# Seven-product pairs at the even places of a job in the second layer of a Fourier, MoE, MoE kernel

## The chip, the cores and the metric

The kernel runs on one core of a Trainium2 chip. The metric is the device time of one execution in microseconds; lower is better.

## What is computed

Two sequences of 3,008 tokens with 256 features go through a Fourier layer (a real FFT along the sequence, a complex 256x256 product with a soft threshold, the inverse FFT). The 6,016 tokens that come out pass two gated layers of the same shape, and the change is in the second of them alone:

```python
h = x @ w_in            # 6016x256 @ 256x2048
relu6 = np.clip(h + 3.0, 0.0, 6.0)
g = h * relu6 / 6.0
return (g @ w_out).astype(np.float32)   # 6016x2048 @ 2048x256
```

The first layer is alike, with `g = h * np.cos(h)`.

## The kernel before

**Precision.** Every fp32 operand is held as a high part (rounded to fp32r) and a low part (the rest). One product of two operands is three matmuls: high weight with high and with low tokens, low weight with high tokens (`three`, L899).

**Jobs and steps.** Each layer is six jobs of tokens (`HALF`: two halves t of 512 tokens each, in the last job 448), and each job is eight steps q = 0 to 7. A step k (0 to 47 in the first layer, 48 to 95 in the second, job jj = k // 8) makes 256 of the 2,048 hidden features for both token halves: four blocks, `ba`, `bd`, `be`, `bc` by feature half f and token half t. The hidden product `x @ w_in` is done with seven products instead of eight (the `mm` calls, 21 matmuls a step), in four PSUM banks `ha` to `hd`. The elementwise work on a block in the second layer is: ACT makes `r` = relu(h + 3) from PSUM (L856), DVE makes `r` = min(r, 6) * h (L864), ACT rounds it to `gh` (L889), POOL or DVE subtracts, `gl` = r - gh (L177 on POOL, L933 on DVE). Between them DVE adds a shared intermediate `p5` to `hb` to get `hd` and `hc` (`add`, L913).

**The output product** accumulates in four PSUM banks a job, `acc{job}_{t}{d}`, for token half t and output half d. An ordinary step costs 24 matmuls for it: four blocks, two output halves, three matmuls. PSUM has two buffers for each d, so the banks of a job are those of the job before, free only after that job's sums were read.

**Seven-product pairs.** At some places the output product of one step's four blocks is done with seven products instead of eight, 21 matmuls instead of 24. `SEVEN` names the places (q = 1, 3, 5 of the second layer's jobs after its first: 15 of them). The work of such a place is spread over three steps. In the *opening* step (E in the code) the blocks' gates are run and the sums of blocks t0 to t2 are formed on DVE (`less`, tile `sums`); in the *closing* step (O) come the sum t3, the high and low parts of the four sums (ACT `sums_hi` L979, POOL `sums_lo` L177) and four of the seven products; three more come in the *tail*, at the head of the step after (P). One product (V4, `old.into`, L1211) goes straight into an accumulator; the four named X1, X2, X3, X5 serve more than one output: each goes to a PSUM bank of its own (`part`, L1003) and DVE keeps its running sum in SBUF tiles `part0` to `part3` (`keep`, L1008). At the end of a job four additions on POOL (`parts_sum`, L1015) combine these tiles, and `finish` (L1024) reads each accumulator once, adds its tile (`o` at L1042) and stores it.

The weights of the seven products are combined once by the converter (`convert`, `pieces`) and stored to DRAM (`ws_dram`); `load_ring` (L949) brings them back for each pair, into halves of the `wo` tiles that the pairs leave unused.

**Order.** The order of the whole loop is written out by hand: each engine runs its instructions in the order in which the code in the step loop (L1132) issues them, with semaphores between engines. `operands` (L457) prepares the next job's tokens in twelve small stages, spread over the steps (`advance`); in the second layer its subtractions `tok` and `st` run on POOL, for job 7 on DVE. `flush` calls `finish` for each half job that has ended.

Of the kernel before, what the change touches and what calls it, by code (L numbers as in the profile page):

```python
# [54 lines left out]
OPERANDS = (1, 2, 2, 2, 2, 3)  # L55
SEVEN = (1, 3, 5)
V11, V12, V22, V1, V2, V3, V4 = range(7)
# [69 lines left out]
def fourier_moe_moe_kernel(ctx, tc, x, w_r, w_i, b_r, b_i, ta, tg, fg, win1, wout1, win2, wout2, out):  # L127
# [54 lines left out]
    w32 = {}  # L182

    def convert(kind, m, c, k):
# [48 lines left out]
        def sums():  # L233
            if kind == "i" and k == 1:
                w = w32[m, c]
                pooled(pool_add, w[:, S1], w[:, A21], w[:, A22])
                pooled(pool_sub, w[:, S3], w[:, A11], w[:, A21])
                yield
                pooled(pool_sub, w[:, S2], w[:, S1], w[:, A11])
                pooled(pool_sub, w[:, S4], w[:, A12], w[:, S2])  # L240
                yield
            if seven and k == 1:
                w = w32[m, c].rearrange("p s f -> p (s f)")[:, :1024].rearrange("p (s f) -> p s f", f=128)
                a11, a21 = a[:, 256:384], a[:, 384:512]
                pooled(pool_add, w[:, V1], a21, w[:, V22])
                pooled(pool_sub, w[:, V3], a11, a21)
                yield
                pooled(pool_sub, w[:, V2], w[:, V1], a11)
                pooled(pool_sub, w[:, V4], w[:, V12], w[:, V2])
                yield  # L250

        def pieces():
# [17 lines left out]
            def store(z, e, cut, rest):  # L270
                for h, t in ((0, cut), (1, rest)):
                    if z < n:
                        sp.dma_start(at[:, h, z:e], f32(t))
                        if seven and k == 0:
                            sp.dma_start(ws_dram[c][:, h, 128:384], f32(t)[:, 1])
                        elif seven:
                            sp.dma_start(ws_dram[c][:, h, 0:128], f32(t)[:, 1, 0:128])
                    else:
                        sp.dma_start(ws_dram[c][:, h, 384:896], f32(t).rearrange("p a f -> p (a f)"))

            if seven and k == 0:
                act.activation(w32[m, c].rearrange("p s f -> p (s f)")[:, 128:384], a[:, 256:512], AF.Copy)
            lows, stores = [], []
            for z in list(range(0, n, 2)) + [2] * (seven and k) + [None, None]:
# [3 lines left out]
                if lows:  # L288
                    low(*lows[0][2:5])
                    if not direct:  # L290
                        stores.append((*lows[0][:2], lows[0][2], lows[0][4]))
                    lows.pop()
                if z is not None:
                    e = min(z + 2, n) if z < n else z + 2
                    part = src[:, z:e] if z < n else w32[m, c][:, 0:4].rearrange("p s f -> p (s f)")[:, 384:896].rearrange("p (s f) -> p s f", f=256)
                    if direct:
# [534 lines left out]
    with tc.manual_schedule(engines=engines):  # L831
# [103 lines left out]
        def seven_at(k):  # L935
            jj, q = divmod(k, STEPS)
            return jj > NJ and q in SEVEN

# [3 lines left out]
        def ring(p, i):  # L942
            if p % 2 == 0 or i < 2:
                return wo_sb[1, i + 4 * (p % 2)][:, :, 1]
# [18 lines left out]
        class Seven:  # L963
# [59 lines left out]

        def finish(jj, t):  # L1024
# [4 lines left out]
            for d in range(2):  # L1029
                a = acc.pop((jj, t, d))  # L1030
# [7 lines left out]
                else:  # L1038
                    to = out[d * 128 : (d + 1) * 128, STARTS[p] + t * n : STARTS[p] + (t + 1) * n]
                    if jj > NJ:  # L1040
                        by = shared()[2][((X1, X3), (X2, X5))[t][d]]
                        dve.scalar_tensor_tensor(o[:, :n], a[:, :n], 1.0 / 6.0, by[:, :n], op0=ALU.mult, op1=ALU.add)  # L1042
                    elif d == 0:
                        act.activation(o[:, :n], a[:, :n], AF.Copy, scale=1.0 / 6.0)
                    else:
                        dve.tensor_scalar(o[:, :n], a[:, :n], 1.0 / 6.0, None, op0=ALU.mult)
                    sp.dma_start(to, o[:, :n])
# [11 lines left out]
        def w_loads(k):  # L1059
# [72 lines left out]
        for k in range(2 * G):  # L1132
            n = HALF[k // STEPS % NJ]
            a, b, c, d = (bank(z, f"h{r}_{k}") for z, r in zip((0, 1, 2, 3) if k % 2 == 0 else (0, 3, 2, 1), "abcd"))
            E, O, P = (k >= i and seven_at(k - i) for i in range(3))
            ba, bd, be, bc = (Block(k, f, t, h) for f, t, h in ((0, 0, a), (0, 1, d), (1, 0, b), (1, 1, c)))

# [215 lines left out]
```

## Time and profile before

| | |
|---|---|
| median of 3 runs | 1145.98 us (1145.41 to 1146.14) |
| the profiled execution | 1145.05 us, its span 1143.3 us |
| PE (matmul) busy | 1135.4 us, 99% of the span, 5300 instructions |
| DVE, ACT, POOL busy | 865.8, 837.4, 850.2 us (76%, 73%, 74%) |
| mean granted TensorE clock | 0.999 |
| second layer | from 661 us to the end |

A row of the timeline has the start and the duration in us, the engine, the line of kernel.py, the operation, out<-in by the program's names without numbers, the shape and the count of equal instructions in a row; in brackets stands how long the engine had been idle before, and what ended that. A tile named `h` with a letter, `acc` or, as output of a matmul, `part` lies in PSUM; all others lie in SBUF.

### The profile page before, as it was taken

To read this page: it belongs to the slowest core of one execution; us is meant where nothing else is said; L and a number is where in the kernel's file an instruction comes from. 1 tells how busy PE (TensorE), PEld (TensorE's weight loads), DVE (VectorE), ACT (ScalarE), POOL (GpSimd) and SP (SyncE) were. 2 spreads that over 40 slices of the span, in tenths; PEclk is the share of its full clock that TensorE was granted. 3 is DMA by queue.
4 is the path that set the end of the run, shared out by engine and by line. 5 is a ranking of instruction groups with operands and counts; after the bars stand their busy time and mean duration, and the time that the engine had idled before them with its cause. 6 is when DMAs were issued, how large, how long until landed. Compare 5 with 4: busy or idle time off the path is not lost.

```text
span 1143.3 us, 16265 instructions
## 1 busy us (share of the span) xinstructions
PE 1135.4 (99%) x5300; PEld 953.5 (83%) x5300; DVE 865.8 (76%) x1261; ACT 837.4 (73%) x1600; POOL 850.2 (74%) x696
## 2 busy tenths in 40 slices
PE   9999999999999999999999999999999999999998
PEld 7888887778888888888889988888888888888897
DVE  5888877886978888888888676666667577576676
ACT  4787788778888888878888876576666567566564
POOL 3557747876987896987887876558867967868764
PEclk9999999999999999999999999999999999999999
DMA  9656968436103023113215520032031041121210
GB/s 230 189 144 176 269 187 304 142 94 207 63 21 134 28 74 120 42 37 134 65 51 196 195 84 19 15 106 65 1 131 40 12 128 33 42 92 34 69 33 33
DMA packets 67621, 115.48 MB, mean 101 GB/s; under 512 B 7488, under 2 KB 41456, under 8 KB 67024
## 3 DMA queue, kind: packets, MB, share of 16 engines
q1 hardware_dynamic: 67408, 114.30, 31.8%
q8 instruction: 42, 0.69, 0.3%
q14 instruction: 43, 0.35, 0.1%
q10 hardware_dynamic: 128, 0.15, 0.0%
HBM read 73.52 MB, written 40.89 MB: 100 GB/s over the span
## 4 chain that ended last, share of the span: by engine, by line
PE 92%; POOL 2%; DVE 1%; DMA 1%; ACT 1%; issue 1%; SPq 0%; POOLq 0%; ACTq 0%
PE acc L901 38%; PE hb L901 16%; PE ha L901 11%; PE pp L657 6%; PE hc L901 5%; PE hd L901 5%; PE part L901 3%; PE bp L686 3%; PE zp L560 2%; POOL gl L177 1%; PE yp L420 1%; PE vp L725 1%; DMA u_dram<-v 1%; DMA x_big<-in_x_dram 1%; POOL st L481 0%
## 5 line engine op out<-in xcount | busy, mean ns | idle before, releaser
L177 POOL TENSOR_TENSOR gl<-r,gh 128x512 fp32r<-128x512 f32 (+1 forms) x337 | 442.6, 1332 | 133.8 <-ACT gh L889 122.6
L901 PE MATMUL acc<-gh,wo 128*128 128x512 f32 (+1 forms) x1342 | 467.0, 386 | 0.0
L901 PEld LDWEIGHTS acc<-gh,wo 128*128 128x128 f32 x1342 | 252.0, 188 | 46.8
L901 PE MATMUL acc<-gl,wo 128*128 128x512 f32 (+1 forms) x671 | 259.0, 386 | 0.6 <-POOL gl L177 0.5
L901 PE MATMUL hb<-tok,wi 128*128 128x512 f32 (+1 forms) x864 | 241.1, 387 | 0.6 <-DVE hd L913 0.6
L889 ACT ACTIVATE gh<-r 128x512 fp32r<-128x512 f32 (+1 forms) x354 | 210.8, 616 | 4.7 <-DVE r L864 2.4
L901 PEld LDWEIGHTS hb<-tok,wi 128*128 128x128 f32 x864 | 160.7, 188 | 32.1 <-DVE hd L913 2.1
L875 ACT ACTIVATE r<-r 128x512 f32<-128x512 f32 (+1 forms) x192 | 118.8, 619 | 62.4 <-DVE r L862 62.4
L901 PE MATMUL ha<-tok,wi 128*128 128x512 f32 (+1 forms) x576 | 160.0, 386 | 1.3 <-ACT yo L439 1.3
L901 PEld LDWEIGHTS acc<-gl,wo 128*128 128x128 f32 x671 | 126.0, 188 | 25.1 <-POOL gl L177 1.7
L913 DVE TENSOR_TENSOR hd<-p,hb 128x512 f32<-128x512 f32 (+1 forms) x96 | 65.7, 684 | 84.1 <-ACT p L1167 43.0
L901 PEld LDWEIGHTS ha<-tok,wi 128*128 128x128 f32 x576 | 107.7, 188 | 22.9 <-ACT yo L439 2.8
L177 POOL TENSOR_TENSOR sums_lo<-sums,sums_hi 128x512 fp32r<-128x512 f32 (+1 forms) x60 | 74.9, 1267 | 67.5 <-PE ha L901 39.3
L1167 ACT ACTIVATE p<-hc 128x512 f32<-128x512 f32 (+1 forms) x96 | 56.4, 587 | 67.0 <-PE hc L901 66.7
L478 POOL TENSOR_TENSOR tok<-st,tok 128x512 fp32r<-128x512 f32 (+1 forms) x77 | 98.1, 1282 | 3.4 <-ACT tok L475 3.4
L901 PE MATMUL hc<-tok,wi 128*128 128x512 f32 (+1 forms) x288 | 79.9, 386 | 0.0
L901 PE MATMUL hd<-tok,wi 128*128 128x512 f32 (+1 forms) x288 | 79.8, 385 | 0.0
L1142 ACT ACTIVATE hb<-ha 128x512 f32<-128x512 f32 (+1 forms) x96 | 55.3, 576 | 30.5 <-PE ha L901 30.3
L913 DVE TENSOR_TENSOR hc<-p,hb 128x512 f32<-128x512 f32 (+1 forms) x96 | 65.3, 680 | 11.4 <-PE hb L901 10.4
L901 PEld LDWEIGHTS hc<-tok,wi 128*128 128x128 f32 x288 | 54.0, 188 | 10.4 <-DVE r L879 0.3
L901 PEld LDWEIGHTS hd<-tok,wi 128*128 128x128 f32 x288 | 54.1, 188 | 10.3
L879 DVE TENSOR_TENSOR r<-r,hb 128x512 f32<-128x512 f32 (+1 forms) x48 | 32.3, 674 | 34.9 <-ACT r L875 34.7
(191 smaller groups left out, 2045.0 us busy)
## 6 DMA issues: line engine op xcount, KB each, us to landing
wo<-ws_dram SPq DMA_DIRECT2D x38, 256.0 KB, 3.3
st<-x_dram SPq DMA_DIRECT2D x18, 512.0 KB, 5.1
rawi<-in_win_dram SPq DMA_DIRECT2D x16, 512.0 KB, 4.0
rawo<-in_wout_dram SPq DMA_DIRECT2D x16, 512.0 KB, 3.9
wi<-wi_dram SPq DMA_DIRECT2D x4, 1792.0 KB, 8.2
u_dram<-v SPq DMA_DIRECT2D x48, 128.0 KB, 2.4
u_sb<-u_dram SPq DMA_DIRECT2D x16, 384.0 KB, 4.1
wo<-wo_dram SPq DMA_DIRECT2D x10, 512.0 KB, 6.3
```

Of the source, the lines that this page charges most:

```text
L177: nc.gpsimd.tensor_tensor(out, x, y, op=ALU.subtract)
L478: subtract(at(lo, t), src, f32(at(hi, t)), op=ALU.subtract)
L560: pe.matmul(zp[:, i * ROWS : (i + 1) * ROWS].rearrange("p (s f) -> p s f", s=2), lhsT=xt[:rows, i, kc * 128 : (kc + 1) * 128], rhs=tt[:row ...
L657: pe.matmul(pp.rearrange("p a e -> p (a e)"), lhsT=za[:, p, kc, 2 * (k2 % 2) : 2 * (k2 % 2) + 2, :].rearrange("p r n -> p (r n)"), rhs=wb[ ...
L686: pe.matmul(bp, lhsT=fgr[:, fi, :], rhs=src[:, :, m, :], start=False, stop=(n == 5), skip_group_check=True)
L875: act.activation(r, r, AF.Sin, bias=math.pi / 2, scale=1.0)
L879: dve.tensor_tensor(r, r, self.h[:, : self.n], op=ALU.mult)
L889: act.activation(gh[:, :n], self.r[:, :n], AF.Copy)
L901: pe.matmul(h[:, :n], lhsT=w, rhs=x, start=start and j == 0, stop=stop and j == 2, skip_group_check=True)
L913: dve.tensor_tensor(h[:, :n], r[:, :n], x[:, :n], op=ALU.add)
L1142: act.activation(b[:, :n], a[:, :n], AF.Copy)
L1167: act.activation(p5[:, :n], c[:, :n], AF.Copy)
```

## The change

The places move from q = 1, 3, 5 to q = 0, 2, 4, 6, in jobs 7 to 10. Job 6, the first of the layer, gets one at q = 6, the last job keeps three (q = 0, 2, 4). That makes 20 places instead of 15, so that in jobs 7 to 10 every even step opens a pair, every odd step closes one, and the tail of a job's last pair lies in the next job's first step. With it go:

- the weight halves that the pairs use (index 0 instead of 1 of `wo`), and a fourth set of combined weights in the converter, from the chunk that stays in SBUF;
- the end of a job: its four `parts_sum` additions all run in the next job's step q = 0, and `finish` is split by output half: `o_00` at the end of step q = 0, the other three within step q = 1 (`turn`);
- the sum t3 (`old.less(3, ...)`) goes from ahead of `add(d, p5, b)` to behind it, in every closing step;
- X1 of a job's first pair is kept by ACT instead of DVE.

```diff
-SEVEN = (1, 3, 5)
+SEVEN = (0, 2, 4, 6)
...
-            return jj > NJ and q in SEVEN
+            return jj >= NJ and q in SEVEN and (jj < 2 * NJ - 1 or q < 6) and (jj > NJ or q == 6)
...
-                if self.k % STEPS == SEVEN[0]:
-                    dve.tensor_scalar(to, h, 1.0 / 6.0, None, op0=ALU.mult)
+                if self.p == 0 or at_k[self.p - 1] // STEPS < self.jj:
+                    if x == X1:
+                        act.activation(to, h, AF.Copy, scale=1.0 / 6.0)
+                    else:
+                        dve.tensor_scalar(to, h, 1.0 / 6.0, None, op0=ALU.mult)
...
-            if k == at_k[0] - 2:
+            if k == at_k[0] - 1:
+                cv.require(("o", 1, 3, 1))
                 load_ring(0)
...
+            turn = k // STEPS > NJ and k % STEPS == 1
...
             if O:
-                old.less(3, old.be.r, old.t(1))
                 advance(k, False)
...
             add(d, p5, b, n)
+            if O:
+                old.less(3, old.be.r, old.t(1))
...
-            flush()
+            if not turn:
+                flush()
...
+            if turn:
+                finish(k // STEPS - 1, 1, range(1))
             ba.second()
...
-            if k // STEPS > NJ and k % STEPS == STEPS - 1:
+            if k == 2 * G - 1:
                 parts_sum(k // STEPS, 0)
-                if k == 2 * G - 1:
-                    parts_sum(k // STEPS, 1)
-            elif k // STEPS > NJ + 1 and k % STEPS == 0:
-                parts_sum(k // STEPS - 1, 1)
+                parts_sum(k // STEPS, 1)
+            elif k // STEPS > NJ and k % STEPS == 0:
+                parts_sum(k // STEPS - 1, 0)
...
                 out_mm(item, range(1, 2))
+                if turn:
+                    finish(k // STEPS - 1, 1, range(1, 2))
...
-            flush()
+            if k // STEPS > NJ and k % STEPS == 0:
+                finish(*ended[0], range(1))
+                parts_sum(k // STEPS - 1, 1)
+            elif turn:
+                finish(*ended[0], range(1, 2))
+                ended.clear()
+            else:
+                flush()
```

**DVE in a closing step.** Before (step 76); `r75_10` is the last block that t3 needs, `sums` its tile:

```order
L933 TENSOR_TENSOR gl75_11_9572<-r75_11_9555,gh75_11_9571 128x512
L933 TENSOR_TENSOR sums_7831<-r75_10_9568,sums_7831 128x512
L913 TENSOR_TENSOR hd_76_9590<-p5_76_9603,hb_76_9588 128x512
L864 SCALAR_TENSOR_TENSOR r76_00_9615<-r76_00_9615,ha_76_9587 128x512
L913 TENSOR_TENSOR hc_76_9589<-p5_76_9603,hb_76_9588 128x512
```

With the change (step 75), from the same place on:

```order
L934 TENSOR_TENSOR gl74_11_9572<-r74_11_9553,gh74_11_9571 128x512
L914 TENSOR_TENSOR hd_75_9590<-p5_75_9602,hb_75_9588 128x512
L934 TENSOR_TENSOR sums_7582<-r74_10_9568,sums_7582 128x512
L865 SCALAR_TENSOR_TENSOR r75_00_9615<-r75_00_9615,ha_75_9587 128x512
L914 TENSOR_TENSOR hc_75_9589<-p5_75_9602,hb_75_9588 128x512
```

The sum t3 and the addition into `hd` have changed places: t3 now stands between that addition and the gate of block 00.

**POOL at the border of jobs 8 and 9** (steps 71 and 72). Before:

```order
L177 TENSOR_TENSOR gl71_11_9223<-r71_11_9173,gh71_11_9222 128x512
L177 TENSOR_TENSOR gl71_10_9234<-r71_10_9185,gh71_10_9233 128x512
L180 TENSOR_TENSOR part1_7835<-part1_7835,part3_7837 128x512
L180 TENSOR_TENSOR part3_7837<-part3_7837,part2_7836 128x512
L177 TENSOR_TENSOR gl72_00_9280<-r72_00_9237,gh72_00_9279 128x512
```

With the change, POOL at the same place:

```order
L177 TENSOR_TENSOR gl71_11_9308<-r71_11_9241,gh71_11_9307 128x512
L177 TENSOR_TENSOR gl71_10_9316<-r71_10_9266,gh71_10_9315 128x512
L180 TENSOR_TENSOR part1_7586<-part1_7586,part0_7585 128x512
L180 TENSOR_TENSOR part2_7587<-part2_7587,part1_7586 128x512
L180 TENSOR_TENSOR part1_7586<-part1_7586,part3_7588 128x512
L180 TENSOR_TENSOR part3_7588<-part3_7588,part2_7587 128x512
L177 TENSOR_TENSOR sums_lo72_0_9398<-sums_7582,sums_hi0_7583 128x512
```

The four additions stand in one run now, behind the last `gl` of the old job and ahead of the first `sums_lo` of the new pair; before, two of them stood there and the other two one step earlier.

**DVE at the same border** (steps 72 and 73). Before:

```order
L864 SCALAR_TENSOR_TENSOR r72_10_9270<-r72_10_9270,hb_72_9200 128x512
L1042 SCALAR_TENSOR_TENSOR o8_00_9283<-acc8_00_8581,part0_7834 128x512
L1042 SCALAR_TENSOR_TENSOR o8_01_9286<-acc8_01_8585,part2_7836 128x512
L913 TENSOR_TENSOR hd_73_9292<-p5_73_9310,hb_73_9290 128x512
L1042 SCALAR_TENSOR_TENSOR o8_10_9320<-acc8_10_8604,part1_7835 128x512
```

With the change, DVE at the same place:

```order
L865 SCALAR_TENSOR_TENSOR r72_10_9357<-r72_10_9357,hb_72_9277 128x512
L934 TENSOR_TENSOR sums_7582<-r72_11_9345,r72_01_9341 128x512
L934 TENSOR_TENSOR sums_7582<-r72_11_9345,sums_7582 128x512
L934 TENSOR_TENSOR gl72_11_9361<-r72_11_9345,gh72_11_9360 128x512
L1045 SCALAR_TENSOR_TENSOR o8_00_9372<-acc8_00_8711,part0_7585 128x512
L914 TENSOR_TENSOR hd_73_9384<-p5_73_9395,hb_73_9382 128x512
L934 TENSOR_TENSOR sums_7582<-r72_10_9357,sums_7582 128x512
```

Three operations of the new pair now stand ahead of `o8_00` at the border. The first matmul of V4 in step 73 writes the bank that `o8_00` frees, and waits for it.

## Rows read from the trace of the kernel before

**Rows 1.** Page, part 1; then from the waits of PE: total, times, longest.

```profile
PE 1135.4 (99%) x5300; PEld 953.5 (83%) x5300; DVE 865.8 (76%) x1261; ACT 837.4 (73%) x1600; POOL 850.2 (74%) x696
...
PE hb L901 <- DVE hd L913: 0.6, 1, 0.6
```

**Rows 2.** Busy time by stretch: PE, PEld, DVE, ACT, POOL (with counts), clock, DMA share.

```profile
900.00:1000.00 100.00, 100.00 (x442) 82.51 (x441) 65.05 (x100) 63.46 (x117) 80.05 (x64) 1.00 0.19 61
```

**Rows 3.** Timeline of PE: the same place of two ordinary steps, 45 matmuls apart.

```profile
703.61 0.84 PE L901 MATMUL hc<-tok,wi 128*128 128x512 f32 x3
...
713.81 0.84 PE L901 MATMUL hc<-tok,wi 128*128 128x512 f32 x3
```

**Rows 4.** Timeline of PE and DVE in closing step 62: a wait of PE.

```profile
806.37 0.97 PE L901 MATMUL hb<-tok,wi 128*128 128x512 f32 x3
...
805.63 0.68 DVE L913 TENSOR_TENSOR hd<-p,hb 128x512 f32<-128x512 f32 x1
```

**Rows 5.** Timeline of DVE and POOL in opening step 75: one DVE operation drawn out.

```profile
942.27 1.27 DVE L933 TENSOR_TENSOR sums<-r,r 128x512 f32<-128x512 f32 x1
...
941.71 1.29 POOL L481 TENSOR_TENSOR st<-st 128x512 f32<-128x512 f32 x1
```

**Rows 6.** Timeline of DVE and POOL, steps 54 to 56: starts close together.

```profile
741.90 0.69 DVE L864 SCALAR_TENSOR_TENSOR r<-r,hb 128x512 f32<-128x512 f32 x1 [0.76 <-ACT r L856]
742.50 1.80 DVE L478 TENSOR_TENSOR tok<-st,tok 128x512 fp32r<-128x512 f32 x1
...
742.46 1.29 POOL L177 TENSOR_TENSOR gl<-r,gh 128x512 fp32r<-128x512 f32 x1 [3.19 <-ACT gh L889]
...
735.83 0.69 DVE L913 TENSOR_TENSOR hd<-p,hb 128x512 f32<-128x512 f32 x1 [1.73 <-PE hb L901]
736.43 1.69 DVE L478 TENSOR_TENSOR tok<-st,tok 128x512 fp32r<-128x512 f32 x1
738.04 0.68 DVE L864 SCALAR_TENSOR_TENSOR r<-r,ha 128x512 f32<-128x512 f32 x1
...
736.28 2.99 POOL L177 TENSOR_TENSOR gl<-r,gh 128x512 fp32r<-128x512 f32 x2 [0.76 <-ACT gh L889]
```

**Rows 7.** Timeline of DVE and POOL, step 51: DVE starts first.

```profile
691.92 0.69 DVE L478 TENSOR_TENSOR tok<-st,tok 128x512 fp32r<-128x512 f32 x1
...
691.98 1.78 POOL L177 TENSOR_TENSOR gl<-r,gh 128x512 fp32r<-128x512 f32 x1 [2.77 <-ACT gh L889]
```

**Rows 8.** Timeline of all engines in closing step 84 (starts at its first `ha`).

```profile
1021.82 0.84 PE L901 MATMUL ha<-tok,wi 128*128 128x512 f32 x3
1027.26 0.39 PE L901 MATMUL part<-gh,wo 128*128 128x512 f32 x1
...
1024.81 0.70 DVE L913 TENSOR_TENSOR hd<-p,hb 128x512 f32<-128x512 f32 x1
1026.05 0.69 DVE L864 SCALAR_TENSOR_TENSOR r<-r,ha 128x512 f32<-128x512 f32 x1 [0.54 <-ACT r L856]
...
1025.36 3.80 POOL L177 TENSOR_TENSOR sums_lo<-sums,sums_hi 128x512 fp32r<-128x512 f32 x3 [3.00 <-issue]
```

**Rows 9.** Timeline of DVE and POOL in closing step 86.

```profile
1044.52 0.69 DVE L913 TENSOR_TENSOR hd<-p,hb 128x512 f32<-128x512 f32 x1
...
1045.03 1.29 POOL L177 TENSOR_TENSOR sums_lo<-sums,sums_hi 128x512 fp32r<-128x512 f32 x1 [2.83 <-ACT sums_hi L979]
```

**Rows 10.** Timeline of PE and POOL, opening step 75 to V4 in step 76; POOL additions in step 79.

```profile
931.17 0.84 PE L901 MATMUL ha<-tok,wi 128*128 128x512 f32 x3
...
945.45 0.39 PE L901 MATMUL acc<-gh,ring 128*128 128x512 f32 x1
...
936.70 2.54 POOL L177 TENSOR_TENSOR gl<-r,gh 128x512 fp32r<-128x512 f32 x2 [0.66 <-ACT gh L889]
...
980.10 2.67 POOL L180 TENSOR_TENSOR part<-part,part 128x512 f32<-128x512 f32 x2
```

**Rows 11.** Timeline of DVE at the border of jobs 8 and 9.

```profile
912.26 1.28 DVE L1042 SCALAR_TENSOR_TENSOR o<-acc,part 128x512 f32<-128x512 f32 x2
```

More of the change, by code (lines that the diff above doesn't have):

```diff
@@ L243, in sums @@
                 w = w32[m, c].rearrange("p s f -> p (s f)")[:, :1024].rearrange("p (s f) -> p s f", f=128)
-                a11, a21 = a[:, 256:384], a[:, 384:512]
+                a11, a21 = a[:, 0:128], a[:, 128:256]
                 pooled(pool_add, w[:, V1], a21, w[:, V22])
@@ L272, in store @@
                     if z < n:
-                        sp.dma_start(at[:, h, z:e], f32(t))
+                        if not direct:
+                            sp.dma_start(at[:, h, z:e], f32(t))
                         if seven and k == 0:
-                            sp.dma_start(ws_dram[c][:, h, 128:384], f32(t)[:, 1])
+                            sp.dma_start(ws_dram[c][:, h, 128:384], f32(t)[:, 0])
                         elif seven:
-                            sp.dma_start(ws_dram[c][:, h, 0:128], f32(t)[:, 1, 0:128])
+                            sp.dma_start(ws_dram[c][:, h, 0:128], f32(t)[:, 0, 0:128])
                     else:
@@ L281, in pieces @@
             if seven and k == 0:
-                act.activation(w32[m, c].rearrange("p s f -> p (s f)")[:, 128:384], a[:, 256:512], AF.Copy)
+                act.activation(w32[m, c].rearrange("p s f -> p (s f)")[:, 128:384], a[:, 0:256], AF.Copy)
             lows, stores = [], []
@@ L289, in pieces @@
                     low(*lows[0][2:5])
-                    if not direct:
+                    if not direct or seven:
                         stores.append((*lows[0][:2], lows[0][2], lows[0][4]))
@@ L295, in pieces @@
                     part = src[:, z:e] if z < n else w32[m, c][:, 0:4].rearrange("p s f -> p (s f)")[:, 384:896].rearrange("p (s f) -> p s f", f=256)
-                    if direct:
+                    if direct and z < n:
                         cut, rest = keep[:, 0, z:e], keep[:, 1, z:e]
@@ L943, in ring @@
             if p % 2 == 0 or i < 2:
-                return wo_sb[1, i + 4 * (p % 2)][:, :, 1]
+                return wo_sb[1, i + 4 * (p % 2)][:, :, 0]
             if len(held) < 1:
@@ L1022, in parts_sum, with finish @@
                     pool_add(to, to, by)
-        def finish(jj, t):
+        def finish(jj, t, ds=range(2)):
             m, p = divmod(jj, NJ)
@@ L1028, in finish @@
                 staged.setdefault("last", persist.tile([128, 2, 2, 512], F32, tag="st", bufs=1, name="st_last"))
-            for d in range(2):
+            for d in ds:
                 a = acc.pop((jj, t, d))
@@ L1039, in finish @@
                     to = out[d * 128 : (d + 1) * 128, STARTS[p] + t * n : STARTS[p] + (t + 1) * n]
[L1040 to L1046, printed above, removed]
+                    by = shared()[2][((X1, X3), (X2, X5))[t][d]]
+                    dve.scalar_tensor_tensor(o[:, :n], a[:, :n], 1.0 / 6.0, by[:, :n], op0=ALU.mult, op1=ALU.add)
                     sp.dma_start(to, o[:, :n])
@@ L1083, in w_loads @@
                 cv.require(("i", 1, 3, 1))
-            elif k == G + 6:
-                cv.require(("o", 1, 3, 1))
         def prepare(k):
```

## The prediction

> **What bounds the kernel now.** I read the page first, then the waits of PE, then busy time by stretch, then the timeline of single steps. PE is busy for 99% of the span, and the longest total that it waits for anything in the second layer is 0.6 us, for DVE's `hd` [rows 1]. By stretch PE is full at a granted clock of 1.00 while DVE, ACT and POOL stand at 63 to 80% [rows 2]. So the second layer takes as long as its matmuls: two equal places of ordinary steps, 45 matmuls apart, lie 713.81 - 703.61 = 10.20 us apart, 0.2267 us a matmul [rows 3]. A matmul that is left out is worth that, as long as everything else stays on time. The reader is to look for what could be late: the instructions that PE waits for have little room in a closing step.
>
> **Removed matmuls.** The order of instructions has 15 matmuls fewer, all with 512 columns: three for each of five more pairs. 15 x 0.2267 = **-3.4 us**. The Trainium skill (TensorE: Matmul & The Clock Gate, Back-to-back issue gap) puts an isolated matmul of 512 columns at about 216 ns; by that the saving would be 3.2 us. The row decides.
>
> **A small wait that goes.** In closing step 62 the matmuls into `hb` that wait for DVE's `hd` take 0.97 us instead of 0.84, and start 0.03 us behind their place [rows 4]. The same stands in steps 70 and 78, since a sum ahead of `hd` was late. With t3 behind `hd` this goes: about 3 x 0.16 = **-0.5 us**. The row also prices any wait of PE for DVE: the matmul starts 806.37 - (805.63 + 0.68) = 0.06 us after DVE's end, and the first one takes 0.13 us longer.
>
> **Who blocks whom on DVE and POOL.** All that follows rests on this. A sum of two SBUF tiles on DVE takes 0.68 us, but in step 75 one took 1.27: POOL was in an operation that ended at 943.00, and the sum ended at 943.54 [rows 5]. It had waited for POOL's whole operation and then needed 0.54 us. In step 56 POOL's `gl` started 0.04 us ahead of such an operation, which DVE issued 0.60 us after the one before it: DVE took 1.80 us [rows 6]. In step 51 DVE was ahead by 0.06 us, and POOL took 1.78 us instead of 1.3 [rows 7]. In these rows the earlier start wins, down to 0.04 us. DVE operations with a PSUM operand (`hd`, gates, `o`) show no such stretching.
>
> **Term A: t3 behind `hd`, in 14 closing steps.** In step 84 DVE starts `hd` 2.99 us after the step's start, and POOL starts its first `sums_lo` at 3.54 [rows 8]. With the change t3, a sum of two SBUF tiles, follows `hd` by 0.60 us: it would start at 3.59, 0.05 us after POOL. In step 86 the same sum gives 0.09 us [rows 9]. POOL's operation runs 3.80 / 3 = 1.27 us, to 4.81; t3 then ends at 5.36, the gate behind it (which starts 0.08 us before that end and takes 0.69) at 5.97. X1's matmuls write the bank that this gate reads; their place is 1027.26 - 1021.82 = 5.44 [rows 8]. With 0.06 us to react and 0.13 us of restart PE loses 5.97 + 0.19 - 5.44 = 0.7 us. The pattern has been seen: in step 55 a two-SBUF operation stands right behind `hd`, POOL starts 0.15 us ahead of it, the operation takes 1.69 us and the gate starts only at 738.04 [rows 6]; there no X1 waits, so it cost nothing. Closing steps with the pattern: 20 less the five in a job's step q = 1 and less the first pair, 14. 14 x 0.7 = **+9.8 us**. Bounds: 0, if DVE gets in first, and 0.7 each. I take the upper end, since both steps have POOL ahead and [rows 6] shows POOL winning with 0.04 us.
>
> **Term B: the border of jobs, five times.** Take step 75 for an opening step (start 931.17) [rows 10]. POOL's last `gl` ends at 8.07. The four additions take 1.33 each (2.67 / 2), so they hold POOL to 13.4; before, POOL was free here after one or three operations. DVE asks for the first of its three two-SBUF operations at 11.1 [rows 5]: the third addition holds it to 12.1, it ends at 12.6. The fourth addition, waiting since 12.1, goes next and ends about 13.9 (a pair of POOL operations with a DVE operation between them takes 2.99 us, 0.45 more than 2.54 [rows 6, 10]). The second sum ends at 14.4, `gl` at 15.0, `o_00` (0.64 [rows 11]) at 15.6. V4 in the next step needs the bank that `o_00` frees; its place is 945.45 - 931.17 = 14.28 [rows 10]. PE loses 15.6 + 0.19 - 14.28 = 1.5 us. Bounds for one border: 0.3 if DVE keeps its turn through all its operations once it has it, 2.8 if POOL's first `sums_lo` also gets ahead of `gl`. I take 1.5, which alternates as [rows 6] does. 5 x 1.5 = **+7.5 us**. While PE stands there, t3, gate and X1 of that step catch up, so term A isn't counted again.
>
> **The first pair (steps 54, 55).** DVE still prepares job 7's tokens there, and one of these operations comes right ahead of `hd` with others in its way. By the length of such an operation, 0.69 us free and 1.7 blocked [rows 6, 7], I put 0 to 1.5 us and take **+0.7 us**.
>
> **Edits at nothing.** The fourth set of weights adds five POOL and two ACT operations in steps 50 to 52, ordinary steps in which POOL has gaps of 3 us [rows 6]; without them the first ring would be late for step 55, more than a step after its loads. 14 more ring loads and 6 more stores go through SP: each pair's ring is loaded a whole step ahead, and the DMA engines are busy 19% of the stretch [rows 2]; the store of `o_00` that now stands ahead of them holds them to the end of the opening step, still some 13 us before V4. POOL gets one operation more per pair, which these steps have room for outside the border. ACT's X1 adds 0.6 us to five closing steps and delays `gl_10`, which had about a microsecond of room.
>
> **Sum.** -3.4 - 0.5 + 9.8 + 7.5 + 0.7 = +14.1 us on the profiled execution's 1145.05 us: 1159.2. The median of the runs is 0.9 us above that execution: **1160.0 us**. By bounds alone the change lies between -3.9 and +9.8 + 14 + 1.5 - 3.9 = +21.4 us.
>
> **Rivals.** A measurement here tells about 0.2% (2.3 us) from no change.
>
> *1. DVE gets ahead of POOL in the closing steps.* A lead of 0.05 to 0.09 us is small, and a POOL start in the profile need not be the moment in which it holds DVE off. Then t3 ends at 4.3, the gate at its old time, and POOL's chain slips half a microsecond, within its room. Only B and the first pair are left: 1145.98 - 3.9 + 7.5 + 0.7 = 1150.3 us. Chance 0.15. The Trainium skill (SBUF — State Buffer, Who interferes with whom) says that issue order decides, and that the first holds the pair of ports for its whole instruction; by that this rival would need DVE's start to come first, which the rows of steps 84 and 86 speak against.
>
> *2. A, and the border costs little.* DVE keeps its turn, 0.3 us a border: 1145.98 - 3.9 + 9.8 + 1.5 + 0.7 = 1154.1 us. Chance 0.10; no row shows two DVE operations in a row ahead of a waiting POOL.
>
> *3. Faster.* DVE starts t3 first and also gets through the border ahead of the additions: the saving stays, 1145.98 - 3.9 + 0.7 = 1142.8 us, 1142.1 if the first pair costs nothing. It decides at two places: t3's start before POOL's `sums_lo` in a closing step (0.05 us), and `o_00`'s end before 14.1 us of an opening step at q = 0. For it speaks that the engines are 20% and more idle [rows 2] and that PE hid all 15 pairs before. Against it speak [rows 5, 6]. Chance 0.20.
>
> *4. Part of each,* ending within 0.2% of before, 1143.7 to 1148.3: 0.05. That the matmuls aren't removed is excluded, the order of instructions shows them gone.
>
> **How the numbers follow.** The forecast, A and B together, has 0.50 and a range of its own of 1154 to 1165 us. Faster is rival 3 (0.20), no change is 4 (0.05), slower is the rest: 0.50 + 0.15 + 0.10 = 0.75. Leaving out rivals 3 and 4 would leave out 0.25, so the range reaches down to 1142; above, 1164 holds the forecast with most of its upper bound.
>
> **What would show it.** Right: in closing steps the `sums` operation behind `hd` lasts about 1.75 us under POOL's first `sums_lo`, and PE's X1 (`part`) has a gap of some 0.7 us; closing steps take 39 x 0.2267 + 0.7 = 9.5 us instead of 8.84. At q = 1 V4's first matmul waits 1.5 us for DVE's `o` line, and two `sums` operations in the step before are drawn out. Wrong: `sums` at 0.68 us in closing steps, with POOL's `sums_lo` at 1.8 instead (rival 1), or PE as full as before with 15 matmuls less (rival 3).

## The result, and the profile after

The changed kernel takes 1162.09 us (median of 4 runs, 1160.93 to 1163.31), the kernel before 1146.06 in the same session: a ratio of 1.0139, 95% interval 1.0127 to 1.0152. The profiled execution took 1160.93 us; its span is 1159.1, 15.8 us more than before. The page and the waits of PE in the second layer (total, times, longest), which answer to [rows 1]:

```profile
span 1159.1 us, 16403 instructions
...
PE 1138.4 (98%) x5285; PEld 949.1 (82%) x5285; DVE 916.3 (79%) x1307; ACT 850.2 (73%) x1621; POOL 876.9 (76%) x710
...
PE part L902 <- DVE r L865: 6.2, 14, 0.6
PE acc L902 <- DVE o L1045: 5.8, 5, 1.2
PE hc L902 <- DVE part L1015: 0.3, 1, 0.3
PE hb L902 <- DVE hd L914: 0.2, 1, 0.2
```

PE has 15 matmuls less and still a longer span: X1 (`part`) waits 14 times for a gate, V4 (`acc`) 5 times for `o`. Before, PE waits nowhere in this layer for as long as 0.05 us: the matmul that waits 0.6 us for `hd` in [rows 1] starts at 236.90 us, in the first layer, and not in the second, as the prediction reads it.

**A closing step.** Timeline of step 59 (starts at 774.73), to set beside [rows 8]:

```profile
777.70 0.70 DVE L914 TENSOR_TENSOR hd<-p,hb 128x512 f32<-128x512 f32 x1 [0.75 <-ACT p L1165]
778.31 1.81 DVE L934 TENSOR_TENSOR sums<-r,sums 128x512 f32<-128x512 f32 x1
780.04 0.68 DVE L865 SCALAR_TENSOR_TENSOR r<-r,ha 128x512 f32<-128x512 f32 x1
...
778.28 4.23 POOL L177 TENSOR_TENSOR sums_lo<-sums,sums_hi 128x512 fp32r<-128x512 f32 x3 [3.83 <-ACT sums_hi L980]
...
780.77 0.50 PE L902 MATMUL part<-gh,wo 128*128 128x512 f32 x1 [0.44 <-DVE r L865]
```

POOL starts 0.03 us ahead of t3 (`sums`), t3 takes 1.81 us instead of 0.68, the gate ends at 780.72, and X1 starts 0.05 later, 6.04 into the step; its place was 5.44. The step lasts 9.60 us instead of 8.84. The same kernel has a step in which it goes the other way, 75:

```profile
944.55 0.68 DVE L934 TENSOR_TENSOR sums<-r,sums 128x512 f32<-128x512 f32 x1
...
944.56 3.09 POOL L177 TENSOR_TENSOR sums_lo<-sums,sums_hi 128x512 fp32r<-128x512 f32 x2 [4.11 <-ACT sums_hi L980]
...
946.17 0.39 PE L902 MATMUL part<-gh,wo 128*128 128x512 f32 x1
```

Here ACT's `p` came 0.28 us later than in step 59 (2.58 us into the step instead of 2.30; the cause stays open). Behind it `hd`, and so t3, came 0.24 us later, ACT's first `sums_hi`, and so POOL, 0.28. So t3 started 0.01 us ahead of POOL, and step 75 lasts 8.84.

**A border.** Steps 64 (starts at 825.23) and 65, to set beside [rows 10]:

```profile
836.34 1.53 DVE L934 TENSOR_TENSOR sums<-r,r 128x512 f32<-128x512 f32 x1
837.78 1.78 DVE L934 TENSOR_TENSOR sums<-r,sums 128x512 f32<-128x512 f32 x1
839.48 0.68 DVE L934 TENSOR_TENSOR gl<-r,gh 128x512 fp32r<-128x512 f32 x1
840.09 0.68 DVE L1045 SCALAR_TENSOR_TENSOR o<-acc,part 128x512 f32<-128x512 f32 x1
...
841.28 1.82 DVE L934 TENSOR_TENSOR sums<-r,sums 128x512 f32<-128x512 f32 x1
...
833.27 5.74 POOL L180 TENSOR_TENSOR part<-part,part 128x512 f32<-128x512 f32 x4
839.60 4.63 POOL L177 TENSOR_TENSOR sums_lo<-sums,sums_hi 128x512 fp32r<-128x512 f32 x3 [0.59 <-ACT sums_hi L980]
...
840.82 0.50 PE L902 MATMUL acc<-gh,ring 128*128 128x512 f32 x1 [1.15 <-DVE o L1045]
...
843.75 0.50 PE L902 MATMUL part<-gh,wo 128*128 128x512 f32 x1 [0.58 <-DVE r L865]
```

POOL's four additions reach to 13.8 us of the opening step, DVE's two sums take 1.53 and 1.78, `o_00` ends at 15.54, V4 starts at 15.59. Then, in the step that has just lost 1.4 us, t3 meets POOL's second `sums_lo` as well, and X1 waits again. Step 81 is the same. In 57 and 73 the two starts lie as close, and t3 gets through; POOL's second `sums_lo` in step 65, then both in step 57:

```profile
841.26 1.28 POOL L177 TENSOR_TENSOR sums_lo<-sums,sums_hi 128x512 fp32r<-128x512 f32 x1
...
758.73 1.85 POOL L177 TENSOR_TENSOR sums_lo<-sums,sums_hi 128x512 fp32r<-128x512 f32 x1
758.75 0.68 DVE L934 TENSOR_TENSOR sums<-r,sums 128x512 f32<-128x512 f32 x1
```

POOL's start is recorded 0.02 us ahead of t3's in both; in 65 t3 takes 1.82 us, in 57 POOL takes 1.85.

**The first pair**, step 56 (starts at 742.15):

```profile
743.55 1.76 DVE L479 TENSOR_TENSOR tok<-st,tok 128x512 fp32r<-128x512 f32 x1
745.23 0.68 DVE L1015 TENSOR_SCALAR part<-part 128x512 f32<-128x512 f32 x1
...
743.47 2.98 POOL L177 TENSOR_TENSOR gl<-r,gh 128x512 fp32r<-128x512 f32 x2
...
745.97 0.98 PE L902 MATMUL hc<-tok,wi 128*128 128x512 f32 x3 [0.26 <-DVE part L1015]
```

Job 7's last token operation stands ahead of DVE's read of X3 and is held up by POOL's `gl`; `hc` waits for the bank.

The step lengths below are read from the first `ha` matmul of a step to that of the next, on PE's timeline. A border is the place where one job ends and the next begins. "Closing" is without the border and the last job, "opening" likewise. The rows from the third on belong to experiments 1, 2, 4, 5, 6, 7, 9, 10 and 12, in this order.

| us | closing | border: 57, 65, 73, 81, 89 | opening | opening at a border: 64, 72, 80 | 55, 56 |
|---|---|---|---|---|---|
| before | 8.83 to 9.03 | none | 10.87 to 10.89 | none | 10.20, 10.20 (no pair) |
| changed | 9.54 to 9.61, one 8.84 | 10.23, 11.21, 10.26, 11.22, 10.29 | 10.88 | 10.88 | 9.65, 11.47 |
| t3 ahead | 8.84 to 9.16 | 11.15, 11.21, 11.20, 11.16, 10.30 | 10.88 | 10.88 | 9.64, 11.47 |
| no additions | 9.51 to 9.60 | 9.55, 9.59, 9.57, 9.58, 8.08 | 10.88 | 10.88 | 9.61, 11.46 |
| POOL later | 8.83 to 8.86 | 10.84, 10.82, 10.83, 10.82, 9.86 | 10.87 to 11.25 | 11.23 | 9.28, 10.88 |
| additions on DVE | 9.51 to 9.62 | 9.53, 9.55, 9.56, 9.53, 8.72 | 10.88 | 11.18 | 9.61, 11.45 |
| t3 last | 8.83 to 8.87 | 10.32, 11.53, 10.41, 13.14, 9.66 | 10.98 to 11.51 | 11.3 | 9.28, 10.88 |
| both mended | 8.83 to 8.85 | 8.84 four times, 8.23 | 11.02 to 11.36 | 11.5 | 9.28, 11.23 |
| t3 by place | 8.85 to 8.88 | 8.84 to 8.86, 8.08 | 10.88 | 11.8 | 9.33, 11.06 |
| all mended | 8.86 to 9.09 | 8.86 to 8.93, 8.51 | 10.88 to 10.90 | 11.5 | 8.88, 10.89 |
| last version | 8.83 to 8.91 | 8.84 to 8.97, 8.08 | 10.88 | 11.2 | 8.86, 10.88 |

### The profile page after: what moved, and what is told of

It reads as the page before. It is cut to its first block, busy times and chain, and to the rows that moved or that the text cites. A ratio compares the mean times of both kernels' runs of the same rounds, so it can differ in the third digit from the quotient of the medians.

```text
span 1159.1 us, 16403 instructions
## 1 busy us (share of the span) xinstructions
PE 1138.4 (98%) x5285; PEld 949.1 (82%) x5285; DVE 916.3 (79%) x1307; ACT 850.2 (73%) x1621; POOL 876.9 (76%) x710
## 4 chain that ended last, share of the span: by engine, by line
PE 88%; DVE 7%; POOL 2%; ACT 1%; issue 1%; ACTq 0%; POOLq 0%; DVEq 0%
PE acc L902 35%; PE hb L902 14%; PE ha L902 10%; PE pp L658 6%; PE hc L902 5%; PE part L902 5%; PE hd L902 4%; PE bp L687 3%; PE zp L561 2%; DVE sums L934 2%; PE yp L421 2%; PE vp L726 1%; POOL gl L177 1%; DVE hd L914 1%; DVE r L865 1%
## 5 line engine op out<-in xcount | busy, mean ns | idle before, releaser
L177 POOL TENSOR_TENSOR gl<-r,gh 128x512 fp32r<-128x512 f32 (+1 forms) x322 | 422.8, 1332 | 132.2 <-ACT gh L890 116.1
L902 PE MATMUL acc<-gh,wo 128*128 128x512 f32 (+1 forms) x1276 | 445.6, 386 | 0.0
L902 PEld LDWEIGHTS acc<-gh,wo 128*128 128x128 f32 x1276 | 239.6, 188 | 44.3
L902 PE MATMUL acc<-gl,wo 128*128 128x512 f32 (+1 forms) x638 | 246.2, 386 | 0.6 <-POOL gl L177 0.5
L890 ACT ACTIVATE gh<-r 128x512 fp32r<-128x512 f32 (+1 forms) x344 | 205.1, 616 | 7.1 <-DVE r L865 4.9
L177 POOL TENSOR_TENSOR sums_lo<-sums,sums_hi 128x512 fp32r<-128x512 f32 (+1 forms) x80 | 111.3, 1408 | 57.1 <-ACT sums_hi L980 35.0
L902 PEld LDWEIGHTS acc<-gl,wo 128*128 128x128 f32 x638 | 119.8, 188 | 24.0 <-POOL gl L177 1.7
L902 PEld LDWEIGHTS hd<-tok,wi 128*128 128x128 f32 x288 | 54.1, 188 | 10.2
```

The costliest lines, as they stand in the source:

```text
L177: nc.gpsimd.tensor_tensor(out, x, y, op=ALU.subtract)
L890: act.activation(gh[:, :n], self.r[:, :n], AF.Copy)
L902: pe.matmul(h[:, :n], lhsT=w, rhs=x, start=start and j == 0, stop=stop and j == 2, skip_group_check=True)
```

## The experiments

In the first four runs the kernel before had a median of 1145.18 us, in the next four 1145.32, in the next three 1146.45, in the last 1145.88. Ratios are to these, with their 95% interval.

**1. t3 ahead of hd again**

```diff
+            early = O and not turn and k != at_k[0] + 1
+            if early:
+                old.less(3, old.be.r, old.t(1))
             add(d, p5, b, n)
-            if O:
+            if O and not early:
                 old.less(3, old.be.r, old.t(1))
```

> The changed kernel with t3 back ahead of the addition into hd, in all closing steps but the five at a border (q = 1) and step 55. Theory (POOL's first sums_lo blocks t3, and t3 holds the gate and X1 back): in the changed kernel's trace eleven of these steps last 9.54 to 9.61 us instead of 8.84, about 0.74 each; all of that goes, the sums of t3 last 0.69 us, and X1 waits for DVE in the three border steps at most. 1162.1 - 11 x 0.74 = 1154.0 us, up to 0.5 more where hd comes 0.16 late as in three steps of before. Rival (with four pairs in a job DVE and POOL are too full, in whatever order t3 stands): the wait moves from X1 to the matmuls behind hd, 0.4 us and more in each closing step, and the time stays at 1160 to 1162.

1155.99 us (1.0092, 1.0077 to 1.0107). In eight of the eleven steps the loss went wholly; in 61, 69 and 77 some 0.3 us stayed, where a token operation of POOL draws out a sum ahead of t3 and `hd` is late. Two border steps, 57 and 73, where nothing was edited, now lost both waits (11.2 us instead of 10.2): POOL's second `sums_lo` is recorded 0.02 us ahead of t3, as in the changed kernel, but here it holds t3 off. These 1.9 us and the 0.9 us of the three steps are why the total is 2 us above the expectation. The price of t3's place stands; that the loss merely moves to `hd` does not.

**2. No additions at the border**

> The changed kernel without the four POOL additions at each of the five borders; the combination of the four running sums at the end of jobs 7 to 10 and 6 is left out, nothing takes its place. Theory (the additions hold POOL in DVE's way): the two sums behind the gates of block 10 in the opening step last 0.7 instead of 1.5 and 1.8 us, o_00 ends near 13.6 us of that step, V4 waits for nothing. The five border steps, which now lose 1.4, 2.4, 1.4, 2.4 and 2.4 us (10.0 in all), lose at most 0.75 each, where t3 meets POOL there too: 1162.1 - 10.0 + (0 to 3.7) = 1152.1 to 1155.8 us. Rival (o_00 is late since three more DVE operations stand ahead of it, POOL apart): V4 still waits about 1 us five times, and the time stays above 1160.

The two `parts_sum` calls at the border are dropped; this kernel leaves out the combination of the running sums there. 1155.51 us (1.0088, 1.0073 to 1.0103). Steps 64 and 65 (64 starts at 824.51):

```profile
835.62 0.68 DVE L934 TENSOR_TENSOR sums<-r,r 128x512 f32<-128x512 f32 x1
836.22 0.68 DVE L934 TENSOR_TENSOR sums<-r,sums 128x512 f32<-128x512 f32 x1
...
837.43 0.68 DVE L1045 SCALAR_TENSOR_TENSOR o<-acc,part 128x512 f32<-128x512 f32 x1
...
838.79 0.39 PE L902 MATMUL acc<-gh,ring 128*128 128x512 f32 x1
```

With the same DVE operations ahead of it `o_00` ends at 13.60, and V4 starts at its place, 14.28. `o_00` reads `part0`, which no addition writes, so it isn't the additions' result that it waited for. So it is POOL's additions that hold DVE's sums up, not DVE's longer queue. What is left at the four 512-wide borders, 9.55 to 9.59, is t3's loss.

**3. The kernel before, with t3 late**

> The kernel before, with the one edit that t3 goes behind the addition into hd; places, borders and matmuls stay. Theory: POOL's first sums_lo starts ahead of t3 in the 512-wide closing steps, 12 of them, and X1 loses 0.74 in each; in the last job's three 448-wide steps the changed kernel's trace shows t3 getting in first, no loss; the three waits for hd of 0.16 go. 1146.0 + 12 x 0.74 - 0.5 = 1154.4 us; less by 0.74 for each step in which t3 happens to start first. Rival (a late t3 hurts only with four pairs in a job): 1145.5 to 1147.

1152.07 us (1.0050, 1.0030 to 1.0069). Closing steps 58 and 60:

```profile
767.29 0.68 DVE L933 TENSOR_TENSOR sums<-r,sums 128x512 f32<-128x512 f32 x1
...
767.31 1.83 POOL L177 TENSOR_TENSOR sums_lo<-sums,sums_hi 128x512 fp32r<-128x512 f32 x1 [7.20 <-PE ha L901]
...
786.95 1.80 DVE L933 TENSOR_TENSOR sums<-r,sums 128x512 f32<-128x512 f32 x1
...
786.92 2.98 POOL L177 TENSOR_TENSOR sums_lo<-sums,sums_hi 128x512 fp32r<-128x512 f32 x2 [2.59 <-issue]
```

In step 58 DVE is 0.02 us ahead and t3 takes 0.68, in step 60 it is 0.03 behind and t3 takes 1.80. Of the 12 steps with 512 columns, DVE is ahead by 0.01 to 0.02 in five (58, 66, 74, 76, 82), and POOL by 0.03 to 0.09 in seven, which last 9.53 to 9.60; step 82 has `hd` late besides and lasts 10.19. The edit alone costs 6.9 us, with three pairs a job and the old borders: the rival that it hurts only with four is out, and the expectation counted five steps too many.

**4. POOL's first sums_lo later**

```diff
-            if O:
-                old.split(0)
...
             elif O:
+                old.split(0)
                 old.split(1)
```

> The changed kernel with t3 still behind hd, but ACT makes r of block 00 ahead of the first sums_hi in each closing step, so that POOL's first sums_lo starts near 4.8 us of the step instead of 3.55. Nothing is added or left out. Theory (who starts first): t3 starts at 3.58 with POOL idle and lasts 0.68, the gate ends at 4.9, X1 at 5.44 doesn't wait, in eleven steps and at the borders: 1162.1 - 11 x 0.74 = 1154 us, down to 1151 if the borders' X1 waits go too; up to 1157 if sums_lo, 1.3 us later, makes the tail's products wait, which would stand as a wait of PE for POOL's sums_lo. Rival (t3's own 0.6 us on DVE ahead of the gate is what X1 waits for): X1 still waits, 1160 to 1162.

1157.33 us (1.0103, 1.0088 to 1.0118). Steps 59 and 60 (59 starts at 775.12):

```profile
778.71 0.69 DVE L934 TENSOR_TENSOR sums<-r,sums 128x512 f32<-128x512 f32 x1
...
779.97 3.81 POOL L177 TENSOR_TENSOR sums_lo<-sums,sums_hi 128x512 fp32r<-128x512 f32 x3 [5.12 <-ACT sums_hi L980]
783.74 1.29 POOL L177 TENSOR_TENSOR gl<-r,gh 128x512 fp32r<-128x512 f32 x1
...
785.09 0.50 PE L902 MATMUL acc<-gl,wo 128*128 128x512 f32 x1
```

t3 at the same place, 0.69 us long: closing steps are 8.83 to 8.86. So t3's own time on DVE isn't what X1 waited for. The price came back in the tail: `gl` of block 10, behind the later `sums_lo`, ends at 785.03, and the matmul that reads it starts at 785.09 instead of 784.87; the step is 0.35 us longer, and fourteen steps with a tail are longer by 4.8 us together. The border steps keep a loss of 2.0 us.

**5. Two border additions on DVE**

```diff
             rest.into(0, 1, V22, rest.operand(3))
+            if k % STEPS == 0:
+                parts_sum(k // STEPS - 1, 0)    # on DVE
...
-            elif k // STEPS > NJ and k % STEPS == 0:
-                parts_sum(k // STEPS - 1, 0)
```

> The changed kernel with the first two of the four border additions on DVE, behind DVE's read of X3 in the opening step, where DVE has idled 2.0 us; POOL keeps two, which then end at 10.7 us of the step, before DVE asks for its first sum at 11.1. Nothing is left out. Theory (POOL's additions block the sums): the two sums last 0.7, V4 doesn't wait at the five borders, and t3 meets POOL there as in other closing steps: the borders lose 0.75 instead of 1.4, 2.4, 1.4, 2.4 and 2.4, as in the run without additions: 1162.1 - 10.0 + 5 x 0.75 = 1155.9 us, up to 1 us more if the two additions delay hd in the opening step. Rival (the length of DVE's queue at the border is what counts): two more DVE operations make V4 wait as long or longer, 1162 and more.

1155.84 us (1.0095, 1.0081 to 1.0109). V4 waits nowhere, though DVE has two operations more; the borders keep t3's loss, and their opening steps take 0.3 us longer.

**6 and 7. t3 behind the read of X1; then with experiment 5's additions**

```diff
-            if O:
-                old.less(3, old.be.r, old.t(1))
...
                 keep()
+                old.less(3, old.be.r, old.t(1))
```

> The changed kernel with t3 behind DVE's read of X1, near 8.2 us of a closing step, when POOL's three sums_lo have ended and its next operation starts at 8.47; the border stays. Theory: no t3 meets POOL ahead of a gate any more, in any closing step: the eleven lose 0.74 less each, step 55 about 0.5 less, the borders keep V4's wait of 1.4 but lose the X1 wait of 1.0 in three of them. 1162.1 - 8.1 - 0.5 - 3.0 = 1150.5 us. If t3 ends too late for the fourth sums_hi and sums_lo, PE waits for POOL's sums_lo in the step after, and the time is above that. Rival (load, not order): 1156 as with t3 ahead, or more.

> t3 behind the read of X1 and two of the border additions on DVE, together. Theory: the two costs are apart and add up; nothing is left of either but what step 55 and 56 lose to job 7's operations on DVE (0.3 and 0.6): 1146.0 - 3.4 (15 matmuls) - 0.5 (the three waits for hd of before) + 0.9 = 1143.0 us, 0.2 to 0.3% under the kernel before. Rival (four pairs in a job leave DVE and POOL too little room, so that a stall that is taken away at one place comes back at the next): 1146 to 1152.

The second kernel has the edits of both, 5 and 6. 1162.34 us (1.0147, 1.0133 to 1.0161) and 1150.46 (1.0042, 1.0028 to 1.0056): both missed. Closing steps are at 8.84, but opening steps grew by up to 0.6 us. Steps 59 and 60 of the second version (60 starts at 782.40):

```profile
781.64 1.14 DVE L934 TENSOR_TENSOR sums<-r,sums 128x512 f32<-128x512 f32 x1
782.70 1.27 DVE L1017 SCALAR_TENSOR_TENSOR part<-part,part 128x512 f32<-128x512 f32 x2
...
780.94 1.29 POOL L177 TENSOR_TENSOR gl<-r,gh 128x512 fp32r<-128x512 f32 x1
...
784.03 0.50 PE L902 MATMUL part<-sums_hi,wo 128*128 128x512 f32 x1
```

With t3 gone from its way POOL's chain ends earlier, and the `gl` that was expected at 8.47 us of the step starts at 7.37: t3 is behind it again, and the reads of X5 and X2 behind t3. X3 needs X2's bank and starts at 784.03, 0.06 us after DVE's read of it. At the borders of experiment 6 a case came up that the prediction held only as a bound; step 64 (starts at 822.86):

```profile
834.41 1.68 DVE L934 TENSOR_TENSOR sums<-r,r 128x512 f32<-128x512 f32 x1
836.02 1.78 DVE L934 TENSOR_TENSOR sums<-r,sums 128x512 f32<-128x512 f32 x1
837.72 1.79 DVE L934 TENSOR_TENSOR gl<-r,gh 128x512 fp32r<-128x512 f32 x1
...
837.69 4.20 POOL L177 TENSOR_TENSOR sums_lo<-sums,sums_hi 128x512 fp32r<-128x512 f32 x3 [0.45 <-ACT sums_hi L980]
...
840.16 0.50 PE L902 MATMUL acc<-gh,ring 128*128 128x512 f32 x1 [2.40 <-DVE o L1045]
```

POOL's `sums_lo` starts 0.03 us ahead of `gl`, which then takes 1.79, and V4 waits 2.4 us instead of 1.2; step 65 lasts 11.53. V4 waits the same 2.4 us in step 81, but that step lasts 13.14. The busy time of PE, PEld, DVE, ACT and POOL, the granted clock and the DMA share in three stretches: the wait in 65, the wait in 81, and what follows in 81:

```profile
838.00:841.00 3.00, 0.84 (x4) 0.71 (x5) 3.00 (x4) 1.43 (x3) 2.97 (x3) 1.00 0.01 5
1002.00:1005.00 3.00, 1.01 (x5) 0.51 (x3) 3.00 (x3) 2.50 (x5) 2.58 (x3) 1.00 0.00 0
1007.00:1009.00 2.00, 2.00 (x6) 1.61 (x5) 0.93 (x2) 0.00 (x0) 0.13 (x1) 0.50 0.84 245
```

Behind the wait in 81 TensorE's granted clock is 0.50, its lower level of 1.2 GHz, for some 3.4 us, and the matmuls come 0.43 us apart instead of 0.23: the other 1.6 us. Behind that in 65 it stays at 1.00. So part of this run's time is the price of the clock, and not of the order of instructions. The two longest of the four runs have a mean granted clock of 0.997 instead of 0.999, which suggests more such falls in them; no trace shows them.

**8. Job 7's last two operations moved**

> The same, and job 7's last two operations on DVE moved: from ahead of hd in step 55 to behind the last gate there, and from the head of step 56 to behind the read of X3. Theory: step 55 lasts 8.84, step 56 10.88; 0.9 us less than the version with both mended: 1142.1 us. Rival: the first pair's extra time has another cause (the weights' conversion, the ring), and stays.

This kernel is that of experiment 7 with two token operations moved. 1150.81 us (1.0048, 1.0035 to 1.0060): a miss. Step 55 fell to 8.84, but the operation moved behind the last gate put t3 behind POOL's `gl` (1.78 us). Step 56 rose to 12.84: PE waits 0.74 us for a DVE read of a bank, behind that t3, and 0.60 for `hd`, behind the other operation and the two additions.

**9 and 10. t3 by its place; the first addition earlier**

```diff
+            if turn:
+                old.less(3, old.be.r, old.t(1))
             add(d, p5, b, n)
...
             add(c, p5, b, n)
+            if O and not turn:
+                old.less(3, old.be.r, old.t(1))
```

> Two border additions on DVE as before, and t3 by its place: ahead of hd at a border (behind o_00, near 2.6 us of the closing step, before POOL's first sums_lo at 3.5), behind the addition into hc in the other closing steps, near 5.65 us, where it waits for POOL's second sums_lo to end at 6.1 and is done by 6.6, early enough for the fourth sums_hi. What failed with t3 behind the read of X1 was that it ended at 9.2 and put off DVE's reads of X5 and X2, whose bank X3 needs in the next step. Theory: closing steps 8.84, opening steps 10.88 again; left over are the opening steps at the border (10.88 + 0.3, hd late behind the two additions, as measured with these additions alone) and 0.9 around the first pair: 1146.0 - 3.4 - 0.5 + 1.4 + 0.9 = 1144.4 us. Rival (four pairs leave too little room on DVE and POOL): a new wait of 0.2 to 0.5 in each pair's steps, 1148 to 1154.

> The same, with the first border addition ahead of DVE's read of X3 (from 1.5 us of the opening step, 2.7 at the latest behind POOL's running operation) instead of behind it, so that hd isn't late behind two of them, and with job 7's last two token operations on POOL instead of DVE. Theory: the border's opening steps take 10.88 (last job 10.48) and steps 55 and 56 8.84 and 10.88: 1.4 + 0.9 us less, 1146.0 - 3.4 - 0.5 = 1142.1 us. Rival: 1144 and more, the first addition makes the read of X3 late and the matmuls into hc wait for it.

The diff is experiment 9's place of t3; it keeps experiment 5's two additions on DVE. Experiment 10 also puts the first of them ahead of the read of X3, and job 7's last two token operations on POOL. 1147.59 us (1.0007, 0.9998 to 1.0016) and 1145.23 (0.9997, 0.9988 to 1.0006), against 1144.4 and 1142.1 expected: both missed, with no difference from the kernel before. Closing and opening steps are at their full speed; the openings at a border are not. Experiment 9, step 64 (starts at 821.43):

```profile
824.28 3.37 DVE L1024 TENSOR_TENSOR part<-part,part 128x512 f32<-128x512 f32 x2
827.58 0.68 DVE L914 TENSOR_TENSOR hd<-p,hb 128x512 f32<-128x512 f32 x1
...
828.31 0.96 PE L902 MATMUL hb<-tok,wi 128*128 128x512 f32 x3 [0.60 <-DVE hd L914]
```

The two additions that took 2.8 us in experiment 5 take 3.4 here, `hd` is 0.6 late. The ten runs of experiment 9 lie between 1145.89 and 1148.84 us and the profile is of one at 1146.26, so what the longer ones lost besides isn't shown. In experiment 10 the earlier addition makes the read of X3 late instead, by 0.35: its rival came true at that place.

**11. The kernel before, with t3 behind hc**

> The kernel before, with t3 behind the addition into hc in its 15 closing steps, nothing else. Theory (t3 there is off everyone's way): the three waits for hd of 0.16 go, nothing is added: 1145.5 us, 0.5 less than before. So the gain of the mended kernel over this one is what the five pairs are worth, 3.4 us. Rival (the mended kernel owes its time to the place of t3, not to its pairs): 1142 to 1143 here too.

1146.56 us (1.0003, 0.9995 to 1.0012). The expected gain of 0.5 us doesn't show, and the interval just allows it; step 82 of the profile, of a run at 1148.20, lost 1.1 us before `hd`. So t3's place alone brings the old pairs little or nothing.

**12. t3 ahead again but at q = 5**

```diff
+            early = O and k % STEPS != 5 and k != at_k[0] + 1
```

> As with all mended, but t3 ahead of hd in the closing steps at q = 1, 3 and 7, and behind the addition into hc only at q = 5 and in step 55. In the run with all mended, t3 behind hc put off POOL's sums_lo by 0.57 us in the step before a border, so that gl started at 1.42 instead of 0.83 in the opening step and held the first border addition on DVE to 2.71; X3's read came late and hc waited. Theory: with t3 ahead POOL starts at 0.83 again, the addition ends near 2.7 and the read of X3 near 3.3, just in time for hc at 3.40: opening steps at the border 10.88 instead of 11.52 to 11.55, step 89 still 0.6 long: 1146.0 - 3.4 - 0.5 + 0.6 = 1142.7 us. Rival (the border keeps a wait in whatever order, since the same sums and additions share one port in those 11 us): opening steps of 11.3 and more, 1144.5 to 1146.

On top of experiment 10, t3 stands ahead of `hd` where `early` holds, and behind `hc` elsewhere. 1144.47 us (0.9986, 0.9977 to 0.9995), the only version whose interval lies below the kernel before, by 0.14%; the 1142.7 expected it misses, and the rival began at 1144.5. Step 64 (starts at 821.95):

```profile
823.36 1.49 DVE L1025 TENSOR_TENSOR part<-part,part 128x512 f32<-128x512 f32 x1
824.77 0.68 DVE L1018 SCALAR_TENSOR_TENSOR part<-part,part 128x512 f32<-128x512 f32 x1
...
825.50 0.96 PE L903 MATMUL hc<-tok,wi 128*128 128x512 f32 x3
```

POOL's `gl` starts at 1.04 us of the step, not 0.83; the addition ends at 2.90, the read of X3 at 3.50, `hc` starts at 3.55 instead of 3.40. The opening steps there are 11.2, between theory and rival. From the start of step 54 to the end of the span this profile has 419.1 us, before 421.3: 2.3 us of the 3.9 that was to be had. By the medians it is 1.4.

## Why the prediction was right, step by step

- *Removed matmuls, the wait for hd.* PE has 15 matmuls less, and the wait for `hd` in steps 62, 70 and 78 is gone. A pair at full pace takes 8.84 + 10.88 us instead of 2 x 10.20, 0.68 less, which is 3.4 for five. The three steps lasted 9.03 instead of 8.84, some 0.6 in all. So -3.4 and -0.5 stand.
- *Who blocks whom.* Right where the starts lie 0.03 us or more apart: in the second layers of all these traces POOL starts 0.03 to 0.15 us ahead of a two-SBUF operation of DVE 108 times (512 wide), and each time holds it off. The Trainium skill (SBUF — State Buffer, Who interferes with whom) says that the order of issue decides; there the traces agree. Closer than that the recorded starts don't tell: of 21 meetings within 0.025 us five go to the one recorded second, steps 57 and 73 of the changed kernel among them. The prediction's remark under rival 1, that POOL's recorded start need not be the moment in which it holds DVE off, is right by these hundredths.
- *Term A.* The mechanism is shown by experiments 1, 3 and 4. The size per step was right, 0.70 to 0.77 against 0.7. The count was not: 11 steps, not 14. In 75, 91 and 93 DVE was first or level with POOL, which the prediction had only as a rival for all steps together. 8.2 us against 9.8.
- *Term B.* The chain came out as forecast: first sum to 12.6, fourth addition to 13.8, second sum to 14.3, `gl` to 14.9, `o_00` to 15.5 (forecast 12.6, 13.9, 14.4, 15.0, 15.6); experiment 2 shows its cause. The step that failed is "term A isn't counted again": in 65, 81 and 89 t3 met `sums_lo` once more, behind V4's wait, and X1 lost another 1.0 us. The wait of PE didn't let t3, gate and X1 catch up there; in 57 and 73 it did only since t3 got through at a recorded lead of POOL of 0.02 us. The five borders cost 1.39 + 2.37 + 1.42 + 2.38 + 2.38 = 9.9 us (steps as listed, less 8.84, the last less 7.91) against 7.5.
- *First pair.* 9.65 - 8.84 and 11.47 - 10.88: 1.4 us against 0.7, near the upper bound. 0.6 of it, the read of X3 behind a token operation in step 56, wasn't in the working.
- *Edits at nothing.* PE waits for no DMA in the second layer; the rings came in time. The trace has 80 loads of rings instead of 60, so 20 more and not 14; nothing in the sum hangs on it.
- *Sum.* -3.4 - 0.5 + 8.2 + 9.9 + 1.4 = 15.6; the spans differ by 15.8, of which 0.3 arose ahead of the second layer. The forecast of 14.1 put A 1.6 too high and B and the first pair 3.1 too low; that these partly offset each other is luck.

## What to carry to other kernels

Where operations of two engines hold each other off, as those of DVE on two SBUF tiles and of POOL do here, and both engines are three quarters busy (79% and 76%), an operation is priced by what runs on the other engine in the moment it is issued, not by its length: 0.68 us became 1.8 by a start 0.03 us too late. Put such an operation where the other engine is known to be idle, and then look where that engine's own chain moves: in experiments 4, 6, 7 and 8 the stall came back one step later. A saving in matmuls is worth its full price only as long as no operation that PE waits for stands behind such a meeting; here 3.9 us that were to be saved became 16 lost.

## What the runs showed of the hardware

- A lead of 0.03 us decides (108 of 108 meetings for POOL; for DVE, whose leads began at 0.05, 14 of 14, with POOL's operation at 1.69 to 1.78 us). Within 0.025 us the profile doesn't tell who wins, and unrelated edits flip it: in experiment 1 two borders where nothing was edited went from 10.2 to 11.2 us.
- Waiting operations took turns: in experiment 6 two sums and `gl` stood on DVE one behind the other and took 1.68, 1.78 and 1.79 us, each behind one operation of POOL. The prediction had taken such turns from two rows [rows 6, 10]. In the second layers of these traces no operation of either engine lasts 2.0 us, so none waited through two of the other's.
- A wait of PE of 2.4 us was followed by a granted TensorE clock of 0.50 for 3.4 us in step 81 of experiment 6, which cost 1.6 us, and by one of 1.00 in step 65. In the 3 us around the two waits PE was busy for 1.01 and 0.84 us.
